# A fused sketch-attention and MLP kernel on one core: another token order, interleaved stages and other engines for the small steps

## The chip, the core and the metric

The kernel runs on one core of a Trainium2 chip. A core has a matrix engine (TensorE, in the profile PE for its matmuls and PEld for its weight loads), a vector engine (VectorE, DVE), an activation engine (ScalarE, ACT), GpSimd (POOL) and SyncE (SP), which here only issues transfers. Each engine works through its own list of instructions in order and waits at an instruction for semaphores. Matmuls write PSUM; DVE and ACT read it, POOL does not in this program. Transfers between HBM and the on-chip SBUF are issued from the queues of SP and ACT. The metric is the device time of one execution in microseconds (us).

## The reference, cut to what matters

Batch 4, heads H = 4, sequence 1088, head size D = 32, sketch size r = 8, model width 128 = H * D, hidden width 512. All data are float32 except S1, S2, w_ch1 and w_ch2, which are float64 and are rounded to float32 on the chip.

```python
def phi(x):
    a = np.einsum('rd,bhsd->bhsr', S1, x)
    b = np.einsum('rd,bhsd->bhsr', S2, x)
    return np.einsum('bhsi,bhsj->bhsij', a, b).reshape(*x.shape[:-1], r * r)
q_p, k_p = (phi(q), phi(k))
kv = np.einsum('bhsf,bhsd->bhfd', k_p, v)
z = np.sum(k_p, axis=2)
num = np.einsum('bhsf,bhfd->bhsd', q_p, kv)
den = np.einsum('bhsf,bhf->bhs', q_p, z)[..., None] + 1e-06
x = (num / den)                      # heads side by side: (batch, 1088, 128)
...
mu = np.mean(x, axis=-1, keepdims=True)
var = np.mean((x - mu) ** 2, axis=-1, keepdims=True)
xn = (x - mu) / np.sqrt(var + 1e-06) * g_ln
ch = np.maximum(xn @ w_ch1, 0.0) @ w_ch2
return (x + ch)
```

## The kernel before, in words

**Tiles.** A batch's 4 x 1088 rows of k or q are loaded as 128 partitions of 34 rows (`load_rows`, L99), v in six transfers a batch (`load_v`, L105). A chunk is 512 tokens of one batch, four tiles of 128; two chunks make 1024 tokens of a batch, and chunk 8 gathers the last 64 tokens of all four batches (two tiles). The order of instructions is written by hand (L547 to L625), and every engine follows it.

**Keys of a batch.** VectorE transposes 32x32 blocks of k into `kT` (`turn_k`, L250). TensorE multiplies by the sketches `sk` (L285, 36 matmul instructions for 9 tiles: each float32 matmul of the program is two instructions in the trace); ACT copies the features from PSUM tile `X` to `fs` (L290). The outer products `kp` (L294) run on GpSimd, those of the first four tiles of batch 0 on VectorE. `key_sums` (L301) forms z by 9 matmuls (L306), a mask (L312), a matmul (L318), and VectorE's copy into the query weights `skq` (L319). `key_values` (L324) contracts `kp` with v in 36 matmuls of 64 columns (L328); `key_spread` (L334) repeats the result over the partitions (ACT L336, PE L341) and VectorE copies it to `kvr` (L346).

**Queries of a chunk.** Transpose (`turn_q`, L262), features with z's denominators (`query_features`, L359, ACT copy L365), quotients on VectorE (L382 to L387), outer products `qp` on GpSimd (L391; chunk 0 on VectorE), a block transpose `qpT` on VectorE (L402), and `numerators` (L408): 32 matmuls of 32x32 weights and 128 columns (L425) into four banks of `X`, copied by ACT to `xT` (L434).

**MLP of a chunk.** `rows_of` (L439) transposes back to token rows `x`; `stats` and `roots` (L449, L460) take the variance on VectorE and 1/sqrt by an ACT square root and five small VectorE operations. `hidden` (L504) multiplies by `w1`, rounded, scaled by g and centred over its rows, in four parts through two PSUM tiles with ACT's ReLU into `hT`; `second` (L512) accumulates `hT` by `w2` into PSUM tile `PO`. `finish` (L521) scales each tile by 1/sqrt on ACT (L526), adds `x` on GpSimd (L529), and SP stores the chunk (L533); chunk 8 has four stores (L540). `weight1` and `weight2` (L477, L492) do the rounding, through `rounded` (L168).

**What sets the order around the change.** In the loop over chunks (L576) a chunk's four hidden matmuls, the numerators of the next chunk and its second matmuls follow one another, with query features two chunks ahead between the first and second hidden matmul; the key work of the next batch stands between chunks.

Of the kernel before, what the change touches and what calls it, by code (L numbers as in the profile page):

```python
# [25 lines left out]
def kernel(  # L26
# [27 lines left out]

    nc = tc.nc
# [24 lines left out]
    XP = ps.tile([P, 512], F32, name="XP")  # L80

# [5 lines left out]
    for i, src in enumerate((S1, S2)):  # L87
        nc.scalar.dma_start(
            out=s_raw[:, D * i : D * (i + 1)],
            in_=bass.AP(src.tensor, src.offset, [[0, P // R], [D, R], [1, D]]),  # L90
        )
# [40 lines left out]
    load_rows(kn, k, 1)  # L132
# [16 lines left out]
    head2 = const([P, H], I32, "head2")  # L149
    pool.iota(head2, [[2, H]], base=1, channel_multiplier=0)  # L150
# [11 lines left out]
    for t in kT:  # L162
        pool.memset(t[:, 8 * P + 64 :], 0.0)
    for t in vn:
        pool.memset(t[64:128, 8 * DM :], 0.0)


    def rounded(dst, raw, last, gain=None):  # L168

        n = raw.shape[-1]
        if raw.dtype == F32:
            last(raw, None)
            return
        words = raw.bitcast(U32)
        lo, hi = words[:, 0 : 2 * n : 2], words[:, 1 : 2 * n : 2]

        def temp(tag, dtype):
            return work.tile([P, n], dtype, tag=f"{tag}{n}", name=tag)  # L180
# [3 lines left out]
        dve.tensor_scalar(out=ex, in0=hi, scalar1=20, scalar2=0x7FF,
                          op0=ALU.logical_shift_right, op1=ALU.bitwise_and)
        dve.tensor_scalar(out=bits, in0=hi, scalar1=0xFFFFF, scalar2=None, op0=ALU.bitwise_and)

        act.activation(exf, ex, AF.Relu, bias=m896)
# [467 lines left out]
```

## Time and profile before

| | us |
|---|---|
| runs (three), median | 164.84 |
| lowest and highest run | 164.75, 166.06 |
| profiled execution, device time | 162.89 |
| its span, first to last instruction | 161.1 |
| PE busy in the span | 117.2 (73%) |
| DVE busy | 83.1 (52%) |
| ACT busy | 53.9 (33%) |
| POOL busy | 44.2 (27%) |
| mean granted TensorE clock | 0.922 |

A profile row names line, engine and operation, then out<-in, shapes and count; behind the bar stand the busy time, the mean ns of one, and the engine's idle time before it with what ended it. The times of engines overlap, so they don't add up to the span. The chain of waits is one path through all engines: it starts at the last instruction and goes back from each to what released it. A granted clock of 1.00 is full rate.

### The profile page before, as it was taken

What the parts mean: (1) busy time and instruction counts of PE and PEld (TensorE: products, weight loads), DVE (VectorE), ACT (ScalarE), POOL (GpSimd) and SP (SyncE); (2) the same over time, 40 slices, a digit from 0 to 9 for tenths busy, and PEclk for the clock granted to TensorE, in tenths of its full rate; (3) what the DMA queues carried; (4) which work ended last, traced back from release to release, by engine and by line L of the source; (5) the groups of instructions that cost most, each with busy time, mean ns of one, the idle gap of its engine ahead of it and who ended that gap; (6) DMA issues with size and microseconds to landing.
All of it is one profiled execution on the core that took longest, in us unless ns stands there. A gap on an engine that the chain in (4) does not pass through costs nothing.

```text
span 161.1 us, 3972 instructions
## 1 busy us (share of the span) xinstructions
PE 117.2 (73%) x1684; PEld 83.0 (52%) x1684; DVE 83.1 (52%) x243; ACT 53.9 (33%) x126; POOL 44.2 (27%) x45
## 2 busy tenths in 40 slices
PE   0047730483499773999999499999979999999700
PEld 0035630151439663549559354964954957669600
DVE  1173148439892638089396605766656666422210
ACT  0501013030615220262563224346245364552510
POOL 4035000004390340562340356333132232020300
PEclk9999999999569969699999857999999999999995
DMA  5998999300000020000020110001102002011020
GB/s 153 322 277 231 371 245 280 63 4 2 0 0 4 0 46 23 0 0 4 6 62 4 12 57 0 4 0 33 38 4 57 12 0 46 23 15 54 8 65 26
DMA packets 7049, 10.28 MB, mean 64 GB/s; under 512 B 2040, under 2 KB 4856, under 8 KB 7032
## 3 DMA queue, kind: packets, MB, share of 16 engines
q1 hardware_dynamic: 5928, 8.92, 20.2%
q10 hardware_dynamic: 1104, 1.11, 2.1%
q8 instruction: 13, 0.21, 0.6%
q14 instruction: 4, 0.03, 0.1%
HBM read 7.80 MB, written 2.23 MB: 62 GB/s over the span
## 4 chain that ended last, share of the span: by engine, by line
PE 60%; DVE 16%; ACT 10%; DMA 3%; issue 3%; POOL 1%; ACTq 1%; DVEq 0%; POOLq 0%
PE HP L509 20%; PE PO L514 14%; PE X L425 6%; PE X L359 5%; PE X L285 5%; DMA s_raw<-in_S_dram 3%; PE XP L443 2%; DVE st L454 2%; PE X L328 2%; ACT sc L526 2%; DVE kT L251 2%; ACT x L445 2%; DVE mv L455 2%; PE X L341 2%; PE PO L489 1%
## 5 line engine op out<-in xcount | busy, mean ns | idle before, releaser
L509 PE MATMUL HP<-xT,w 128*128 128x512 f32 (+1 forms) x72 | 38.1, 655 | 0.7 <-ACT hT L510 0.7
L514 PE MATMUL PO<-w,hT 128*128 128x128 f32 x272 | 34.0, 278 | 0.0
L514 PEld LDWEIGHTS PO<-w,hT 128*128 128x128 f32 x272 | 31.8, 192 | 1.5 <-issue 1.4
L510 ACT ACTIVATE hT<-HP 128x512 f32<-128x512 f32 (+1 forms) x36 | 20.4, 574 | 16.6 <-PE HP L509 16.6
L391 POOL TENSOR_TENSOR qp<-a,fq 128x1024 f32<-128x1024 f32 (+1 forms) x8 | 14.7, 1844 | 39.1 <-DVE a L387 25.1
L285 PE MATMUL X<-sk,kT 128*64 128x64 f32 x144 | 8.8, 296 | 19.2 <-DVE kT L251 14.7
L529 POOL TENSOR_TENSOR ob<-sc,x 128x512 f32<-128x512 f32 x8 | 10.1, 1266 | 44.7 <-issue 23.7
L509 PEld LDWEIGHTS HP<-xT,w 128*128 128x128 f32 x72 | 13.0, 209 | 13.4 <-ACT hT L510 7.0
L294 POOL TENSOR_TENSOR kp<-fs 128x2304 f32<-128x2304 f32 (+1 forms) x4 | 14.8, 3709 | 12.6 <-ACT fs L290 12.6
L285 PEld LDWEIGHTS X<-sk,kT 128*64 128x64 f32 x144 | 7.4, 199 | 21.1 <-DVE kT L251 13.4
L454 DVE BATCH_NORM_STATS2 st<-x 128x6 f32<-128x128 f32 x34 | 9.1, 268 | 14.3 <-ACT x L445 14.3
L382 DVE TENSOR_TENSOR ac<-fq 128x128 f32<-128x128 f32 (+1 forms) x9 | 4.7, 521 | 22.4 <-ACT fq L365 22.4
L526 ACT ACTIVATE sc<-PO,rstd 128x128 f32<-128x128 f32 x34 | 9.7, 367 | 11.2 <-DVE st L454 7.1
L402 DVE STREAM_TRANSPOSE qpT<-qp 128x1024 f32<-128x1024 f32 (+1 forms) x9 | 10.6, 1181 | 2.2 <-POOL qp L391 2.1
L425 PEld LDWEIGHTS X<-qpT,kvr 32*32 32x32 f32 x640 | 7.3, 106 | 8.3 <-issue 6.1
L359 PEld LDWEIGHTS X<-skq,qT 128*64 128x64 f32 x128 | 6.7, 160 | 7.8 <-DVE qT L265 3.8
L469 DVE TENSOR_TENSOR r<-r,r 128x4 f32<-128x4 f32 (+1 forms) x9 | 10.5, 1166 | 0.3
L425 PE MATMUL X<-qpT,kvr 32*32 32x128 f32 (+1 forms) x640 | 10.4, 275 | 0.0
L445 ACT COPY x<-XP 128x512 f32<-128x512 f32 (+1 forms) x9 | 5.1, 562 | 15.2 <-PE XP L443 15.2
L359 PE MATMUL X<-skq,qT 128*64 128x96 f32 x128 | 8.5, 284 | 1.8 <-DVE qT L265 1.2
L290 ACT COPY fs<-X 128x256 f32<-128x256 f32 (+1 forms) x8 | 3.2, 397 | 15.8 <-PE X L285 15.8
L489 PE MATMUL PO<-gw,ones 128*128 128x512 f32 x2 | 2.1, 1141 | 8.4 <-DVE gw L485 8.4
(76 smaller groups left out, 116.5 us busy)
## 6 DMA issues: line engine op xcount, KB each, us to landing
kn<-in_k_dram SPq DMA_DIRECT2D x4, 544.0 KB
qn<-in_q_dram SPq DMA_DIRECT2D x4, 544.0 KB
vn<-in_v_dram SPq DMA_DIRECT2D x16, 128.0 KB
out_dram<-ob SPq DMA_DIRECT2D x8, 256.0 KB
w_raw<-in_moe_w_ch_dram ACTq DMA_DIRECT2D x2, 512.0 KB
vn<-in_v_dram SPq DMA_DIRECT2D x8, 16.0 KB
out_dram<-ob SPq DMA_DIRECT2D x4, 32.0 KB
s_raw<-in_S_dram ACTq DMA_DIRECT2D x2, 32.0 KB
```

What stands on the lines that cost most here:

```text
L285: pe.matmul(X[64 * c : 64 * c + 64, base + W2R * t : base + W2R * (t + 1)], kT[b % 2][:, P * t + 64 * c : P * t + 64 * c + 64], sk, start= ...
L294: eng.tensor_tensor(out=_ap(o, 0, P, H * F * t0, [[F, (t1 - t0) * H], [R, R], [1, R]]), in0=_ap(f, 0, P, W2R * t0, [[2 * R, (t1 - t0) * H] ...
L359: pe.matmul(X[64 * i : 64 * i + 64, 1024 + WQ * t : 1024 + WQ * (t + 1)], src[:, P * t + 64 * i : P * t + 64 * i + 64], w, start=True, sto ...
L391: eng.tensor_tensor(out=_ap(p, 0, P, 0, [[F, m], [R, R], [1, R]]), in0=_ap(a2, 0, P, 0, [[R, m], [1, R], [0, R]]), in1=_ap(f, 0, P, R, [[R ...
L402: dve.transpose(_ap(t, 0, P, 0, [[32, n], [32 * n, 8], [1, 32]]), p[:, 0 : n * H * F])
L425: pe.matmul(X[D * h : D * h + D, o : o + 32 * m], kv[rows, DM * i + D * h : DM * i + D * h + D], t[rows, src : src + 32 * m], start=(i == ...
L454: dve.bn_stats(out=st[:, 6 * t : 6 * t + 6], in_=x[c][:, P * t : P * (t + 1)])
L469: dve.tensor_tensor(out=r1, in0=r1, in1=r0, op=ALU.mult)
L509: pe.matmul(hp[:, 0:n], w1[:, P * j : P * (j + 1)], xT[c][:, 0:n], start=True, stop=True)
L510: act.activation(hT[c][:, 512 * j : 512 * j + n], hp[:, 0:n], AF.Relu)
L514: pe.matmul(PO[:, DM * t : DM * (t + 1)], hT[c][:, 512 * j + P * t : 512 * j + P * (t + 1)], w2[:, DM * j : DM * (j + 1)], start=(j == 0), ...
L526: act.activation(sc[:, P * t : P * (t + 1)], PO[:, P * t : P * (t + 1)], AF.Copy, scale=rstd[c][:, t : t + 1])
```

## The change

**Token order.** A partition's 34 rows are now two runs of 17. A tile of 128 takes every run's t-th token, so kT, qT, v and the output use runs of 17: each 512-column transpose becomes two of 256 that write every second column, v comes in two transfers a batch, and the last tile is token 16 of each run.

**First chunk.** S1 and S2 are issued on two queues, w1 and w2 on SP behind batch 0. Three fill matmuls of zeros run at the start. Key products are all GpSimd's, in pieces; quotients of chunk 0 read PSUM; w1's low words go over ACT and GpSimd, and a matrix `center` (identity less 1/128) does the centring in one matmul.

**z on four tiles.** `key_sums` uses four column tiles of 32 instead of two of 64. **Numerators by batch.** From batch 1 on 32 matmuls serve both chunks, with 256 columns. **Powers on GpSimd.** 1/sqrt is an add and a power of -0.5. The quotient products go to GpSimd too; a ninth column of the sums holds 1e-6. **Residual on DVE.** Scale and add are one VectorE operation a tile, from PSUM. **New slots.** The order is written as two functions, `odd` and `even`, that put key and query work of the next batch between the MLP's matmuls.

```diff
-        for r in range(4):
-            nc.sync.dma_start(
-                out=_ap(vn[b], 32 * r, 32, 0, [[8 * D, H], [1, 8 * D]]),
...
+        for e in range(2):
+            n = (8 + e) * D
+            nc.sync.dma_start(
+                out=_ap(vn[b], 64 * e, 64, 0, [[NT * D, H], [1, n]]),
+                in_=bass.AP(v.tensor, base + 8 * e * D, [[U * D, 64], [S * D, H], [1, n]]),
...
+    load_s(nc.sync, 0, S1)
+    load_s(nc.scalar, 1, S2)
+    nc.scalar.dma_start(out=g_raw, in_=moe_g_ln.rearrange("(p o) -> p o", o=1))
     load_rows(kn, k, 0)
-    nc.scalar.dma_start(out=w1_raw, in_=moe_w_ch1)
     load_rows(qn, q, 0)
     load_v(0)
+    nc.sync.dma_start(out=w1_raw, in_=moe_w_ch1)
+    load_rows(kn, k, 1)
...
+    def turn(dst, off, src, t0, n):
+        for u in range(2):
+            dve.transpose(
+                _ap(dst, 0, P, off + u, [[64, 2], [P, n], [2, 32]]),
+                _ap(src, 0, P, U * D * u + D * t0, [[8 * D, 2], [D, n], [1, D]]),
+            )
...
         for t in range(NT):
-            c = t % 2
+            c = t % 4
             pe.matmul(
-                X[64 * c : 64 * c + 64, 1536:1568],
+                bank(bn, 32 * c, 32, 0, [[1, HR]]),
...
+        eng = pool if bn is None else dve
+        eng.tensor_tensor(
+            out=_ap(ac, 0, P, 0, [[9, m], [1, R]]), in0=_ap(f, 0, P, 0, groups),
...
+    def numerators(b, c0, c1):
+        src = qpT[b]
+        o, n = P * (c0 % 2), P * (c1 - c0)
...
+        pool.tensor_scalar(out=va[:, 0:n], in0=_ap(mv, 0, P, 1, [[2, n]]), scalar1=EPS,
+                           scalar2=None, op0=ALU.add)
+        pool.tensor_tensor(out=rs[:, 0:n], in0=va[:, 0:n], in1=half_power[:, 0:n], op=ALU.pow)
...
+        dve.scalar_tensor_tensor(
+            out=obs[c][:, P * t : P * (t + 1)],
+            in0=PO[:, P * t : P * (t + 1)] if src is None else src[:, 0:P],
+            scalar=rstd[c][:, t : t + 1], in1=x[c][:, P * t : P * (t + 1)],
+            op0=ALU.mult, op1=ALU.add,
+        )
...
+    fill(3, 512)
     turn_k(0, 0, 4)
+    key_features(0, 0, 4, 0)
...
+    def odd(b):
+        c, m = 2 * b + 1, b + 1
...
+        hidden(c, 0)
+        if m < B:
+            key_spread(m, 0)
+        hidden(c, 1)
+        hidden(c, 2)
+        hidden(c, 3)
+        if keys:
+            key_features(m + 1, 0, 4, 2)
+            key_features(m + 1, 4, NT, 3)
+            turn_q(2 * m + 2)
+            turn_q(2 * m + 3)
+        second(c, 0)
+        if keys:
+            key_sums(m + 1, 1)
...
+        second(c, 2)
+        last = 2 * m + (2 if m < B else 1)
+        numerators(m, 2 * m, last)
+        numerators_out(2 * m)
+        second(c, 3)
+        rows_of(2 * m)
...
+    def even(b):
+        c, m = 2 * b, b + 1
+        hidden(c, 0)
+        hidden(c, 1)
+        query_features(2 * m, 2)
...
+        hidden(c, 2)
+        hidden(c, 3)
+        if m < B:
+            query_features(2 * m + 1, 3)
...
+        rows_of(c + 1)
+        second(c, 0)
+        second(c, 1)
+        query_turn(2 * m)
+        stats(c + 1)
+        if m < B:
+            key_values(m, 1)
+            key_values_out(1)
+        second(c, 2)
+        second(c, 3)
```

How the instructions stand at three places. A row has the line, the operation, out<-in with the program's names (a number behind a name tells buffers apart), the size and a count.

TensorE from the first key values to the first hidden matmuls, before:

```order
L328 MATMUL X<-kp_190,vn_85 32x64 x36
L341 MATMUL X<-ident,kvT 128x128 x2
L359 MATMUL X<-skq_180,qT 64x96 x8
L489 MATMUL PO<-gw,ones 128x512
L425 MATMUL X<-qpT,kvr_194 32x128 x32
L443 MATMUL XP<-ident,xT 128x128 x4
L359 MATMUL X<-skq_180,qT 64x96 x8
L509 MATMUL HP_70<-xT,w_198 128x512
L285 MATMUL X<-sk,kT_149 64x64 x18
L509 MATMUL HP_71<-xT,w_198 128x512
```

The same stretch after:

```order
L410 MATMUL X<-skq,qT 64x32 x8
L410 MATMUL XP<-skq,qT 64x3x32 x8
L376 MATMUL X<-kp_176,vn_83 32x64 x36
L391 MATMUL X<-ident,kvT 128x128 x2
L628 MATMUL PO<-gw,center 128x512
L489 MATMUL X<-qpT,kvr_180 32x128 x32
L327 MATMUL PO<-sk,kT_133 64x2x32 x8
L547 MATMUL HP_70<-xT,w_184 128x512
L510 MATMUL XP<-ident,xT 128x128 x4
L547 MATMUL HP_71<-xT,w_184 128x512
```

The query features of chunks 0 and 1 now stand ahead of the key values, and the first eight key features of batch 1 ahead of the first hidden matmul.

VectorE in the first batch, from the key transposes on, before:

```order
L251 STREAM_TRANSPOSE kT_148<-kn_77 128x4x4x32 x2
L257 STREAM_TRANSPOSE kT_148<-kn_77 128x64
L236 TENSOR_TENSOR s2b<-s_f,m_140 128x128
L294 TENSOR_TENSOR kp_190<-fs_188 128x1024
L312 TENSOR_TENSOR zT<-X,m_140 128x32
L319 COPY skq_180<-X 128x4x8
L265 STREAM_TRANSPOSE qT<-qn_81 128x4x4x32
L346 COPY kvr_194<-X 128x256
```

And after:

```order
L287 STREAM_TRANSPOSE kT_132<-kn_75 128x2x4x32 x4
L293 STREAM_TRANSPOSE kT_132<-kn_75 128x2x32
L287 STREAM_TRANSPOSE qT<-qn_79 128x2x4x32 x4
L357 TENSOR_TENSOR zT<-X,m_124 128x32
L603 TENSOR_SCALAR g_187<-g_raw 128x1
L604 TENSOR_SCALAR g_188<-g_raw 128x1
L209 TENSOR_SCALAR ex<-w_raw 128x512
L368 COPY skq<-X 128x32
L217 TENSOR_SCALAR bits<-w_raw 128x512
L434 TENSOR_TENSOR ac_140<-fq,X 128x16x8
```

Key products and the copy of kvr have left VectorE, four half transposes of q came ahead of zT, and three steps of w1's rounding stand between zT and the copy of z's weights into skq.

TensorE in the steady stage, an odd chunk (chunk 1) with the keys of batch 2, before:

```order
L509 MATMUL HP_70<-xT,w_198 128x512
L359 MATMUL X<-skq_181,qT 64x96 x8
L509 MATMUL HP_71<-xT,w_198 128x512
L509 MATMUL HP_70<-xT,w_198 128x512
L509 MATMUL HP_71<-xT,w_198 128x512
L425 MATMUL X<-qpT,kvr_195 32x128 x32
L514 MATMUL PO<-w_199,hT 128x128 x8
L443 MATMUL XP<-ident,xT 128x128 x4
L514 MATMUL PO<-w_199,hT 128x128 x8
L306 MATMUL X<-fs_188 64x32 x9
L318 MATMUL X<-zT,s2b 128x32
```

And after:

```order
L547 MATMUL HP_70<-xT,w_184 128x512
L547 MATMUL HP_71<-xT,w_184 128x512
L327 MATMUL X<-sk,kT_132 64x2x32 x18
L552 MATMUL PO<-w_185,hT 128x128 x4
L352 MATMUL X<-fs_174 32x32 x9
L552 MATMUL PO<-w_185,hT 128x128 x4
L366 MATMUL X<-zT,s2b 128x32
L552 MATMUL PO<-w_185,hT 128x128 x4
L489 MATMUL X<-qpT,kvr_181 32x256 x32
L552 MATMUL PO<-w_185,hT 128x128 x4
L510 MATMUL XP<-ident,xT 128x128 x4
```

The key steps that stood between chunks now stand between the four parts of the second matmul, and the numerators have twice the columns and come once for two chunks.

More of the change, by code (lines that the diff above doesn't have):

```diff
@@ L203, with fill @@
     warm = const([P, 1], F32, "warm")
-    act.activation(warm, one, AF.Sqrt)
-    s_f = const([P, 2 * D], F32, "s_f")
-    def s_last(mant, scale):
-        if scale is None:
-            dve.tensor_copy(out=s_f, in_=mant)
-        else:
-            dve.tensor_tensor(out=s_f, in0=mant, in1=scale, op=ALU.mult)
-    rounded(s_f, s_raw, s_last)
+    act.activation(warm, one, AF.Relu)
+    def fill(n, cols):
+        for _ in range(n):
+            pe.matmul(PO[:, 0:cols], zeros[:, 0:P], zeros[:, 0:cols], start=True, stop=True)
@@ new lines, with round_s @@
+    s_f = const([P, 2 * D], F32, "s_f")
+    def round_s():
+        if s_raw.dtype == F32:
+            dve.tensor_copy(out=s_f, in_=s_raw)
+            return
+        r = Rounded(s_raw, "s")
+        r.exponent()
+        r.mantissa()
+        r.scale()
+        dve.scalar_tensor_tensor(out=r.mant, in0=r.lo, scalar=2.0**-52, in1=r.mant,
+                                 op0=ALU.mult, op1=ALU.add)
+        dve.tensor_tensor(out=s_f, in0=r.mant, in1=r.e3.bitcast(F32), op=ALU.mult)
+    round_s()
@@ new lines @@
+    query_features_out(1, XP_BANK)
+    query_quotients(0, 2)
+    query_products(0, 2, 4)
+    query_products(0, 0, 2, 2)
+    key_values_out(1)
+    key_spread(0, 0)
+    if weight1:
+        weight1.scale()
+        weight1.product(gw)
+    else:
+        dve.tensor_scalar(out=gw, in0=w1_raw, scalar1=g_raw, scalar2=None, op0=ALU.mult)
+    query_turn(0, 0, 2)
+    query_turn(0, 2, 4)
+    pe.matmul(PO, center, gw, start=True, stop=True)
+    numerators(0, 0, 1)
+    numerators_out(0)
+    act.copy(w1, PO)
@@ L569 @@
+    turn_k(1, 0, 4)
+    key_features(1, 0, 4, PO_BANK)
+    query_quotients(1)
+    query_products(1, 0, 4)
+    if weight2:
+        weight2.exponent()
+        weight2.mantissa()
+        weight2.low()
+        weight2.low_added()
+        weight2.scale()
+        weight2.product(w2)
+    else:
+        pool.tensor_copy(out=w2, in_=w2_raw)
     turn_k(1, 4, 4)
     turn_k_rest(1)
[L571 to L586 removed]
+    query_turn(1)
@@ L629 @@
+    odd(0)
+    for b in range(1, B):
+        even(b)
+        odd(b)
+    for j in range(JC):
+        hidden(8, j)
+    second(8, 0)
+    finish(8, 0)
+    second(8, 1, XP)
+    finish(8, 1, XP)
+    for b in range(B):
+        store_rest(b)
 _INS = ["q", "k", "v", "S1", "S2", "moe_g_ln", "moe_w_ch1", "moe_w_ch2"]
```

598 lines of the change are left out of this document (306 added, 292 removed).

## The prediction

> **What bounds the kernel now.** I read the granted clock and the engines' busy time by stage first, cut where the chain of waits changes its character: until chunk 0's transposed features are written, until chunk 1's first hidden matmul, until chunk 8's first hidden matmul, and the tail. A row has the stretch, its length, the busy time (and count) of TensorE's matmuls, its weight loads, VectorE, ACT and GpSimd, the granted clock, the DMA engines' share and GB/s.
>
> ```profile
> 0.00:34.44 34.44, 12.74 (x214) 9.27 (x214) 14.74 (x39) 5.64 (x11) 5.56 (x25) 1.00 0.80 227
> 34.44:65.48 31.04, 21.46 (x313) 15.83 (x313) 19.52 (x53) 8.76 (x20) 10.58 (x5) 0.81 0.04 10
> 65.48:148.22 82.74, 79.01 (x1135) 54.62 (x1135) 47.23 (x145) 36.33 (x84) 26.75 (x14) 0.95 0.08 21
> 148.22:161.10 12.88, 4.02 (x26) 3.27 (x24) 1.62 (x6) 3.17 (x11) 1.26 (x1) 0.82 0.12 31
> ```
>
> Stage three is TensorE's: 79.0 of 82.7 us. Stages one and two take 65.5 us and use TensorE for 34.2; no engine is full there, so a chain of latencies sets them. The chain of waits, in order of time (start, length, what), shows it, and gives the price of each step; of its 328 pieces, these:
>
> ```profile
> 0.74 0.63 ACTq L88
> 1.41 5.59 DMA s_raw<-in_S_dram
> 9.16 0.63 DVE kT L251
> 9.84 1.15 PE X L285 x16
> 11.43 1.39 PE X L285 x20
> 12.84 0.43 ACT fs L290
> 15.87 2.19 PE X L328 x72
> 19.83 0.43 DVE kvr L346
> 26.39 0.32 DVE ex L184
> 30.23 2.07 PE PO L489 x2
> 32.31 1.47 PE X L425 x63
> 33.80 0.59 ACT xT L434
> 40.31 0.72 ACT exf L188
> 43.77 4.46 PE HP L509 x6
> 54.42 0.42 PE X L318 x2
> 63.00 0.71 PE X L285 x16
> 79.62 2.87 PE HP L509 x6
> 82.49 1.00 PE X L425 x56
> 83.49 1.98 PE PO L514 x16
> 85.47 0.44 PE XP L443 x4
> 87.69 1.19 PE X L328 x72
> 89.39 0.72 PE X L341 x4
> 108.37 0.84 PE X L359 x16
> ...
> 143.01 1.39 PE X L425 x98
> ```
>
> Three things to see. S lands at 7.0 and nothing runs until then. From 20.3, where kvr ends, to 34.4 one thing follows another: query features, their quotients, then (26.4) the rounding of w1, then (30.2) the centring matmul, then numerators. And the first stage's matmuls run at about half rate although its clock reads 1.00: sixteen key-feature matmuls take 1.15 us at 9.84 and 0.71 at 63.00, 72 key-value matmuls 2.19 against 1.19, and six hidden ones 4.46 at 43.77 against 2.87 at 79.62.
>
> **Start of the change: S to key values.** Both halves of S are issued on ACT's queue, beside kn on SP's. The change puts one on each, ahead of kn. An undisturbed small transfer is bounded by SyncE's wait for the last stores:
>
> ```profile
> SPq L651 <- DMA out_dram<-ob: 3.6, 2, 3.0
> ```
>
> So S lands between 7.0 (no gain) and 0.74 + 0.63 issue + 3.0 = 4.4; I take 4.4, since nothing of size is ahead of it. The rounding to sk keeps its 2.1 us (7.0 to 9.16): 6.5. The transposes become halves with every second column written; no row shows that form. These do bound it:
>
> ```profile
> L265 DVE STREAM_TRANSPOSE qT<-qn 128x512 f32<-128x512 f32 x8 | 5.5, 694 | 0.0
> L271 DVE STREAM_TRANSPOSE qTr<-qn 128x64 f32<-128x64 f32 x4 | 0.8, 202 | 0.0
> L391 POOL TENSOR_TENSOR qp<-a,fq 128x1024 f32<-128x1024 f32 x7 | 13.7, 1954 | 37.9 <-DVE a L387 25.1 <-DVE r L467 12.8
> L391 DVE TENSOR_TENSOR qp<-a,fq 128x1024 f32<-128x1024 f32 x1 | 1.2, 1224 | 0.0
> L391 POOL TENSOR_TENSOR qp<-a,fq 128x512 f32<-128x512 f32 x1 | 1.1, 1067 | 1.2 <-DVE r L467 1.2
> ```
>
> A line through 202 ns at 64 and 694 at 512 gives 0.41 us for 256; the ends are 0.35 (half the long one) and 0.69 (stride costs a factor two). Taken 0.41: 0.8 for the first pair, 7.3. The three fill matmuls are six instructions of 1.04 (30.23: 2.07 for two) from about 1.2, so TensorE is free at 7.4, just in time; their worth is that the key matmuls run at the warm rows. Then 0.71 and the copy (8.5), twenty more at 0.89 and the copy (9.9), the first query features beside it, 18 sums at the key features' warm rate (0.8; four column tiles taken as no gain, the ends are 0.2, all four at once, and 1.3, the cold rate of 9.84) to 10.8, zT 0.2, the 0.42 of z's weights: 11.4. Then VectorE must copy z's weights, behind w1's first rounding steps. Here the change adds a risk. All four key products go to GpSimd: three of 1.07 and one of some 1.5 (line through the two GpSimd rows), 8.5 to 13.2, where VectorE took the first 1024 columns (1.2) beside GpSimd with the rest. And the timeline shows what a running GpSimd instruction does to VectorE:
>
> ```profile
> 44.32 4.15 POOL L294 TENSOR_TENSOR kp<-fs 128x2304 f32<-128x2304 f32 x1
> 45.73 2.77 DVE L457 TENSOR_SCALAR va<-mv 128x4 f32<-128x4 f32 x1
> 54.04 0.17 DVE L457 TENSOR_SCALAR va<-mv 128x4 f32<-128x4 f32 x1
> ```
>
> The same small operation takes 0.17 alone and 2.77, until GpSimd ends, beside it. So w1's first steps, 0.6 alone by what w1's exponent takes at 26.39, cost up to 2.4 (until the last key product); taken 1.2: 12.6. They also need w1, which moves to SyncE's queue behind kn, qn and v of batch 0: 2.2 MB at stage one's 227 GB/s land it at 10.5, a microsecond ahead; kn and v come well before their use. Query features (1.1), key values 1.19, copy 0.4, spread 0.72, copy 0.4: kvr at 16.4 (was 20.3).
>
> GPSIMD Engine Reference (the Trainium skill, Key points and Engine selection) says that GpSimd shares its SBUF interfaces with VectorE, in contention when a VectorE instruction uses two ports or two SBUF inputs, and that elementwise work is about twice as fast on VectorE. It speaks against these moves. The rows agree on the blocking; for the speed they show 1954 against 1224 ns, and by the page's factor of two on 1224 the four pieces would end at 14.1 instead of 13.2, some 0.4 into the key values, an estimate that would make the sum 133.4.
>
> **First chunk to its features.** Quotients and half the products of chunk 0 now read PSUM beside the key values. w1: exponent, mantissa and low part on ACT (0.7 each from 12.4: 14.5), then GpSimd's sum (1.3), half of chunk 0's products (1.07), VectorE's two scale steps squeezed between (0.7), the product 1.3: 18.8. Centring 1.1 to 2.1, numerators 1.1 to 1.5, copy 0.59: 22 to 23; I take 23.5 with something for a cold clock (was 34.4; ends 20 and 28).
>
> **Chunk 0 to chunk 1.** Before, chunk 0's later hidden matmuls waited until 43.8 behind batch 1's keys, whose transposes stood late on VectorE and whose copies stood behind w2's rounding on ACT; after that statistics, z, query features, products and spread of batch 1 followed one another until 65.5. Now TensorE's work in this stretch is: w1 copy 0.6, key features 1.6, hidden 3.8, rows 0.9, sums 0.8, z 0.4, numerators 1.1, second 4.0, query features 1.7, key values 1.2: 16.1. I add 1.6 for a cold clock (4.46 less 2.87) and 1.8 because w2's three ACT passes stand ahead of the first ReLU: 19.5. Chunk 1 starts at 43.0 instead of 65.5.
>
> **The steady stage.** From 79.0 busy: a mean clock of 0.95 is 8 us at half rate, 4.1 lost if TensorE was busy in all of it; less 2.8, since in part it waited. Numerators for 256 columns once a batch instead of 128 twice, 64 instructions either way. The wide form has no row: it costs 1.0 if the rate of instructions limits it, 2.0 if the columns do. The 128 narrow ones of chunk 8, 32 columns each, speak for the first: 1.39 at 143.01 for 98 of them, 14 ns apart, against 1.00 for 56, 18 apart, at four times the columns. Taken 1.07: less 2.9 in three batches (0 to 3.0). Query features of chunk 3 leave (-0.8), keys of batch 2 and a spread come in (+1.6, +0.7): 74.8. What stands between is hidden work: scaling (34 ACTIVATEs) and the residual (eight GpSimd adds) become 34 VectorE operations of 128 elements (0.2 to 0.7, the rows of 64 and 512; some 0.3), which take 10 us of VectorE's 35 idle ones, and lengthen the wait for the PSUM bank by no more than the four scalings did; roots leave ACT and VectorE for two GpSimd instructions a chunk; the quotient products go to GpSimd, some 0.4 each by its line. Two new waits per batch (keys' second half behind the first copy, rows behind the numerators' copy): 0.5 each, 2 in all: 77.
>
> GpSimd's power of 128x4 has no row: the nearest is VectorE's 0.17 for 128x4, the far end GpSimd's 1.95 us for a whole query product. Its result is due some 8 us later, so either costs nothing.
>
> **Tail.** The last four stores are issued from 154.18 on; the span ends at 161.1.
>
> ```profile
> L526 ACT ACTIVATE sc<-PO,rstd 128x128 f32<-128x128 f32 x34 | 9.7, 367 | 11.2 <-DVE st L454 7.1 <-PE PO L514 4.1
> 154.18 2.22 SPq L540 DMA_DIRECT2D out_dram<-ob  x4
> ```
>
> Four stores go out one after the other; now two on each of two queues: -1.1. The last ReLUs no longer stand behind four scalings of 0.37 on ACT, which overlap a little (-1.1), and two scalings and an add become one short operation (-0.7): 10.
>
> **Sum.** 23.5 + 19.5 + 77 + 10 = 130.0 against 161.1. The profiled execution took 162.89, 1.8 more than its span: 131.8. The median of the runs, 164.84, is 1.2% above the profiled one: 133.
>
> **The rivals.** (1) The start stays long: GpSimd's run of products holds w1's and w2's rounding on VectorE, and the clock falls back. For it: the 2.77 row, and clock 0.81 in stage two. Each of the four stretches of VectorE rounding waits up to 2.4 (+6), and 16 us of TensorE work at half rate adds up to 5 more than I put in; against: most of it overlaps. With two thirds of it: 140. TensorE: Matmul & The Clock Gate (the Trainium skill, Part 1) has the clock fall to half after an idle window of about 3.4 us and return after a busy one; by that rule, a fill that ends at 7.4 would not outlast the wait for w1. No run here shows the fill; the half-rate rows agree. (2) The steady stage is not TensorE's: the interleaved slots wait for ACT and GpSimd, as the 31 us of stage two did. At 2.5 us a batch and 1 us a chunk: +12, 144. Against it: ACT and GpSimd are under half busy there. (3) Everything overlaps, the clock stays up: 19 for stage one, 17 for two, 75, 9: 123. (4) Not faster: the strided half transposes. Ten stand ahead of the first key values and features, eight a batch later, and no row has their form. Each extra us of one costs 9 or so at the start. In the steady stage VectorE is busy 47 of 83 us, 14 of a batch's 24. At about 2.2 us apiece (1.8 more than taken) the start loses 16, and a batch gains 14 on VectorE, 4 more than there is room for, 13 in three: the 30 saved are gone, 163. Below that the kernel is faster. Against it: this is five times the line through the rows.
>
> **How the numbers follow.** My forecast (128 to 138) 0.55; rival (1) 0.20; (2) 0.11; (3) 0.08; (4) 0.06. The range 126 to 143 leaves out (4), half of (3) and the worse half of (2). All but (4) lie far below 163, so faster by over 1%, about what a measurement of this kernel can tell, 0.93; within 1% 0.02; slower 0.05.
>
> **What would show it.** S landing near 4; the first key features at 0.7 for sixteen; chunk 0's features copied near 23 and chunk 1's first hidden near 43; 32x256 numerators at 1.1 us for 64; a TensorE row of nines from 43 to the end; a DVE transpose of 128x256 near 0.41. A transpose over 1 us, VectorE rounding rows over 1 us, or hidden matmuls of chunk 0 at the rate of 43.77 would show me wrong.

## The result and the profile after

The changed kernel takes 138.06 us (median of four runs, 136.94 to 138.93) where the kernel before took 164.8 beside it: a ratio of 0.840, 95% interval 0.830 to 0.850. The profiled execution took 136.94, with a span of 135.2, 1.7 around it. The ratios leave out executions that were disturbed (two of s_one_queue's four, its profiled one among them, of which only the first 10 us are read, two of residual_on_act's, and three of the kernel before beside the last four kernels); the medians do not.

First the granted clock and busy time by stage of the changed kernel, cut at the prediction's four places (columns as there: stretch, length, TensorE's matmuls, its weight loads, VectorE, ACT, GpSimd, clock, DMA share, GB/s).

```profile
0.00:26.52 26.52, 16.64 (x252) 9.69 (x252) 13.87 (x45) 7.08 (x15) 14.38 (x30) 0.83 0.93 272
26.52:43.85 17.33, 16.51 (x273) 12.06 (x273) 7.64 (x28) 8.07 (x15) 9.47 (x9) 0.87 0.17 37
43.85:124.66 80.81, 75.08 (x973) 54.10 (x968) 34.28 (x124) 29.14 (x56) 34.68 (x39) 0.96 0.08 25
124.66:135.20 10.54, 3.85 (x24) 3.08 (x23) 2.44 (x10) 1.89 (x5) 0.95 (x2) 0.92 0.16 39
```

Against before the stages lose 7.9, 13.7, 1.9 and 2.3 us: the gain is made ahead of chunk 1's first hidden matmul. Against the forecast of 23.5, 19.5, 77 and 10 they are off by +3.0, -2.2, +3.8 and +0.5. The longer of the two misses can be seen in the page's picture of the span in 40 slices (tenths of TensorE's busy time, and of its granted clock):

```profile
PE   5963924699999923899999989999999999999900
PEclk9999595559999996589999999999999999999997
```

The 15th and 16th slice (47 to 54 us) hold a 2 and a 3 in the middle of the nines, and the clock reads 6, 5 and 8 from the 16th to the 18th. The chain of waits names what ended late there (start, length, what):

```profile
42.42 0.23 POOL va L524
...
42.73 1.02 POOL rstd L526
43.75 0.44 POOL ac L434
...
45.36 1.95 POOL qp L456
47.31 0.42 POOL ac L434
...
48.91 1.96 POOL qp L456
...
50.90 1.25 DVE qpT L469
52.14 0.66 DVE kT L287 x2
...
52.85 1.15 PE X L327 x16
...
55.78 2.01 PE PO L552 x8
```

Chunk 1's hidden matmuls are done at 48.1 and TensorE wants batch 2's key features next. Their rows (kn, long landed) are to be transposed by VectorE, where that stands behind the transposes of chunk 2's and chunk 3's products; and those wait for two rounds of quotients and products, one after the other on GpSimd, behind chunk 1's power. TensorE is idle for 4.75 us, and what follows runs at half rate (called cold here, and full rate warm): 1.15 us for sixteen key features (0.69 elsewhere), 2.01 for eight second-layer matmuls (1.09 at 61.94). From 63.47 on, the chain is TensorE's almost alone.

The timeline of the start shows the other miss (start, length, engine, line, what; in brackets the idle time before it and what ended it):

```profile
11.99 1.20 DVE L209 TENSOR_SCALAR ex<-w_raw 128x512 uint32<-128x512 uint32 x1 [0.35 <-DMA w_raw<-in_moe_w_ch_dram]
...
17.46 0.29 DVE L434 TENSOR_TENSOR ac<-fq,X 128x128 f32<-128x128 f32 x1 [3.84 <-PE X L376]
...
19.51 0.37 ACT L383 COPY kvT<-X 128x256 f32<-128x256 f32 x1 [3.74 <-DVE qp L456]
...
22.36 2.08 PE L628 MATMUL PO<-gw,center 128*128 128x512 f32 x2 [1.71 <-POOL gw L239]
```

The quotients of chunk 0, whose features were there at 14.0, start when the last key-value matmul (L376) ends; the key values' copy, whose matmuls ended at 17.4, starts when VectorE's product ends; and the weights gw, whose scale steps stand behind those quotients, end at 22.3.

### The profile page after: what moved, and what is told of

Read it like the earlier page. It is cut to its first block, busy times and chain, and to the rows that moved or that the text cites. A ratio compares the mean times of both kernels' runs of the same rounds, so it can differ in the third digit from the quotient of the medians.

```text
span 135.2 us, 3549 instructions
## 1 busy us (share of the span) xinstructions
PE 112.1 (83%) x1514; PEld 78.9 (58%) x1514; DVE 58.2 (43%) x206; ACT 46.2 (34%) x90; POOL 59.5 (44%) x79
## 4 chain that ended last, share of the span: by engine, by line
PE 70%; DVE 7%; POOL 6%; DMA 6%; ACT 2%; SPq 2%; issue 1%; ACTq 0%; DVEq 0%; POOLq 0%
PE PO L552 23%; PE HP L547 21%; PE X L489 6%; DMA w_raw<-in_moe_w_ch_dram 6%; PE X L410 4%; PE X L376 3%; PE XP L510 3%; PE X L327 3%; POOL qp L456 3%; PE PO L628 2%; POOL gw L239 1%; SPq L119 1%; DVE qpT L469 1%; PE XP L410 1%; SPq L110 1%
## 5 line engine op out<-in xcount | busy, mean ns | idle before, releaser
L547 PE MATMUL HP<-xT,w 128*128 128x512 f32 (+1 forms) x72 | 34.7, 602 | 0.1
L340 POOL TENSOR_TENSOR kp<-fs 128x768 f32<-128x768 f32 (+3 forms) x12 | 17.9, 1512 | 9.6 <-ACT fs L332 9.6
L564 DVE SCALAR_TENSOR_TENSOR ob<-PO,rstd,x 128x128 f32<-128x128 f32 x33 | 9.2, 338 | 22.7 <-issue 14.7
L501 ACT COPY xT<-X 128x512 f32<-128x512 f32 (+1 forms) x9 | 5.1, 564 | 23.6 <-PE X L489 23.6
L327 PE MATMUL X<-sk,kT 128*64 128x64 f32 x108 | 5.4, 259 | 6.4 <-DVE kT L287 5.0
L526 POOL TENSOR_TENSOR rstd<-va,half_power 128x4 f32<-128x4 f32 (+1 forms) x9 | 8.9, 994 | 0.7
L489 PE MATMUL X<-qpT,kvr 32*32 32x256 f32 (+2 forms) x448 | 8.5, 320 | 0.3 <-DVE skq L368 0.3
L410 PEld LDWEIGHTS X<-skq,qT 128*64 128x64 f32 x128 | 5.3, 137 | 5.4 <-ACT hT L548 3.0
L410 PE MATMUL X<-skq,qT 128*64 128x96 f32 (+2 forms) x128 | 6.6, 246 | 1.9 <-DVE skq L368 1.3
L521 DVE BATCH_NORM_AGGREGATE mv<-st 128x2 f32<-128x6 f32 x34 | 6.2, 182 | 1.2
L191 PE MATMUL PO<-zeros 128*128 128x512 f32 x6 | 5.5, 1088 | 1.4 <-DVE bit L164 1.4
```

What stands on the lines that cost most here:

```text
L327: pe.matmul(bank(bn, 64 * c, 64, HR * (t - t0), [[HR * n, 2], [1, HR]]), kT[b % 2][:, P * t + 64 * c : P * t + 64 * c + 64], sk, start=Tru ...
L340: pool.tensor_tensor(out=_ap(o, 0, P, H * F * t0, [[F, n], [R, R], [1, R]]), in0=_ap(f, 0, P, HR * t0, [[R, n], [1, R], [0, R]]), in1=_ap( ...
L410: pe.matmul(bank(bn, 64 * i, 64, P * s0 + HR * t, [[P, s1 - s0], [1, HR]]), src[:, P * t + 64 * i : P * t + 64 * i + 64], skq[:, w + HR * ...
L489: pe.matmul(bank(r, D * h, D, o + o2, [[1, m]]), kv[rows, DM * i + D * h : DM * i + D * h + D], src[rows, 256 * (2 * h + i) + o + o2 : 256 ...
L526: pool.tensor_tensor(out=rs[:, 0:n], in0=va[:, 0:n], in1=half_power[:, 0:n], op=ALU.pow)
L547: pe.matmul(hp[:, 0:n], w1[:, P * j : P * (j + 1)], xT[c][:, 0:n], start=True, stop=True)
```

## The experiments

Twelve kernels. The first three are edits of the changed kernel, three_orders is all three together, and the other eight are edits of three_orders. They ran in three groups, the first on one chip and the other two on another (medians of before: 164.73, 163.75, 163.29), so the ratio to before is the better comparison between groups; a difference of 0.01 in it (1.6 us) is the least that stands out.

| kernel | median us | ratio to before (95%) |
|---|---|---|
| changed kernel | 138.06 | 0.840 (0.830 to 0.850) |
| keys2_ahead | 131.39 | 0.801 (0.793 to 0.809) |
| w1_ahead | 133.15 | 0.811 (0.803 to 0.820) |
| kv_own_bank | 133.48 | 0.813 (0.806 to 0.821) |
| three_orders | 126.47 | 0.771 (0.764 to 0.778) |
| no_fill | 126.69 | 0.775 (0.769 to 0.781) |
| narrow_numerators | 127.82 | 0.782 (0.776 to 0.788) |
| residual_on_act | 132.39 | 0.803 (0.795 to 0.812) |
| further_orders | 126.05 | 0.771 (0.764 to 0.777) |
| s_one_queue | 130.60 | 0.795 (0.787 to 0.804) |
| twice_turned | 132.59 | 0.815 (0.809 to 0.821) |
| further_orders2 | 125.35 | 0.771 (0.766 to 0.777) |
| powers_on_act | 141.29 | 0.868 (0.862 to 0.874) |

### keys2_ahead: the hole is VectorE's order

```diff
     stats(1)
+    turn_k(2, 0, 4)
+    turn_k(2, 4, 4)
+    turn_k_rest(2)
+    turn_q_rest(0)
+    turn_q_rest(1)
     query_quotients(2)
...
     query_turn(3)
-    turn_k(2, 0, 4)
-    turn_k(2, 4, 4)
-    turn_k_rest(2)
-    turn_q_rest(0)
-    turn_q_rest(1)
```

> The transposes of batch 2's key rows stand on DVE ahead of chunk 2's quotients and no longer behind chunks 2 and 3's product transposes. Theory A (DVE's order makes TensorE's hole of 4.75 us at 48.1 to 52.9, since those transposes stand behind two serial chains of quotients and products on GpSimd): key features of batch 2 start within 0.5 us of chunk 1's last hidden matmul, the hole, its 0.5 us after the first copy and the half-rate work behind it (about 2 us) go, and the time is 130 to 133. Rival B (GpSimd's chain is late for everything): the hole moves to batch 1's numerators, which need chunk 3's products transposed at 52.1, or to the key sums, and the time is 135 to 138.

Theory A held: 131.39. TensorE's timeline, from chunk 1's last hidden matmul on:

```profile
47.66 0.69 PE L327 MATMUL X<-sk,kT 128*64 128x64 f32 x16
48.82 0.80 PE L327 MATMUL X<-sk,kT 128*64 128x64 f32 x20 [0.47 <-ACT fs L332]
...
53.23 0.41 PE L366 MATMUL X<-zT,s2b 128*128 128x32 f32 x2 [1.13 <-DVE zT L357]
...
54.54 1.50 PE L489 MATMUL X<-qpT,kvr 32*32 32x256 f32 x64
```

The key features follow without a wait and at the full rate. The 0.47 behind the first copy, which theory A had going, stays, and a smaller wait of 1.13 for z comes up; the numerators, which rival B saw waiting for chunk 3's products, don't wait. GpSimd's chain was late only for what had been queued behind it.

### w1_ahead and kv_own_bank: the two waits of the start

w1_ahead moves the scale and product of w1's rounding ahead of chunk 0's quotients, and the centring matmul ahead of the spread:

```diff
         weight1.low_added()
+        weight1.scale()
+        weight1.product(gw)
     query_features_out(1, XP_BANK)
     query_quotients(0, 2)
     query_products(0, 2, 4)
     query_products(0, 0, 2, 2)
+    pe.matmul(PO, center, gw, start=True, stop=True)
     key_values_out(1)
     key_spread(0, 0)
-    if weight1:
-        weight1.scale()
-        weight1.product(gw)
...
-    pe.matmul(PO, center, gw, start=True, stop=True)
```

> The scale and the last product of w1's rounding stand ahead of chunk 0's quotients and products on DVE and GpSimd, and the centring matmul ahead of the spread key values on TensorE. Theory A (w1's rounding, behind the quotients, ends the wait before the first numerators): weights gw end near 18 in place of 22.3, the centring runs in TensorE's idle stretch, the numerators start near 21.3, xT(0) is written near 23.3 in place of 26.5, and the time falls by 2.5 to 3.5 to about 135. Rival B (the quotients, which wait for the key values, end it by themselves): xT(0) not before 25 and the time falls by less than 1.5. Rival C (chunk 0's early gain is lost at the hole before batch 2's key features, because that hole is timed by the statistics of chunk 1 and GpSimd): xT(0) moves but the time by under 1.

kv_own_bank leaves the order and gives batch 0's key values and their spread other PSUM tiles:

```diff
-    BANKS = [(X, 0), (X, 512), (X, 1024), (X, 1536), (PO, 0), (XP, 0)]
+    BANKS = [(X, 0), (X, 512), (X, 1024), (X, 1536), (PO, 0), (XP, 0), (HP[0], 0), (HP[1], 0)]
...
-    key_values(0, 1, 0, 4)
-    key_values(0, 1, 4, NT)
+    key_values(0, 6, 0, 4)
+    key_values(0, 6, 4, NT)
...
-    key_values_out(1)
-    key_spread(0, 0)
+    key_values_out(6)
+    key_spread(0, 7)
```

> Batch 0's key values and their spread go into the two hidden banks, idle until chunk 0's hidden matmuls, in place of the four-bank tile that the quotients read. Theory A (chunk 0's quotients wait for the key values' last matmul, 3.84 us, and the key values' copy for the DVE products, 3.74 us, only because all sit in one PSUM tile): the first quotient starts at 14 to 15.5 in place of 17.46, the copy of the key values at 17.5 in place of 19.51, the numerators 1.5 to 3 earlier, the time 135 to 136.5. Rival B (the quotient waits for the matmuls in any case, by TensorE's order): it still starts after 17.3 and the time stays within 0.7 of the changed kernel.

Both theories held, and both gains, 4.9 and 4.6 us between the medians, came out larger than expected; between the profiled spans they are 3.9 and 3.0. The timelines, first of w1_ahead, then of kv_own_bank:

```profile
18.19 1.13 PE L623 MATMUL PO<-gw,center 128*128 128x512 f32 x2 [1.06 <-POOL gw L239]
...
20.92 1.07 PE L489 MATMUL X<-qpT,kvr 32*32 32x128 f32 x64 [0.46 <-ACT kvr L395]
...
48.37 1.01 PE L327 MATMUL X<-sk,kT 128*64 128x64 f32 x16 [4.77 <-DVE kT L287]
```

```profile
14.58 0.29 DVE L434 TENSOR_TENSOR ac<-fq,X 128x128 f32<-128x128 f32 x1 [0.50 <-PE X L410]
...
17.94 0.37 ACT L383 COPY kvT<-HP 128x256 f32<-128x256 f32 x1 [1.62 <-PE HP L376]
```

In w1_ahead xT(0) is written at 22.6 in place of 26.5. 1.4 us of the excess are TensorE's rate: the centring takes 1.13 instead of 2.08 and the numerators 1.07 instead of 1.47, with shorter waits ahead of them. The hole keeps its length (4.77) and shifts by the whole 4.5 us, so rival C, that it would swallow the gain, falls. In kv_own_bank the quotient waits for its own matmuls (L410) and the copy for the key values: the waits were for the tile X, not for data. Both edits cut the same stretch, so their gains should not add, and they don't: the next version gains 11.6, as much as keys2_ahead and w1_ahead together.

### three_orders

> All three of the edits before. If the start is bound by the two waits and the middle by DVE's order, as the theories say: xT(0) written at 21 to 23.5, no hole above 1 us after chunk 1's hidden matmuls, time 126 to 130. If the start's gain is lost in a later wait (rival): no better than the transposes alone, within 1 us of it.

126.47, inside the first theory's band; one wait above 1 us is left after chunk 1's hidden matmuls, the 1.13 for z. The stages, cut at the same places as above:

```profile
0.00:22.31 22.31, 15.49 (x252) 10.12 (x252) 13.61 (x45) 7.06 (x15) 13.18 (x30) 0.85 0.92 272
22.31:39.05 16.74, 14.97 (x272) 10.77 (x272) 9.15 (x35) 7.88 (x15) 10.63 (x10) 1.00 0.42 107
39.05:114.15 75.10, 72.98 (x973) 52.08 (x967) 32.53 (x118) 29.16 (x56) 34.64 (x39) 1.00 0.08 27
114.15:124.80 10.65, 4.02 (x26) 3.25 (x24) 2.56 (x10) 1.90 (x5) 0.95 (x2) 0.85 0.15 38
```

From chunk 1 on TensorE is busy for 73.0 of 75.1 us at clock 1.00: the forecast's steady stage (74.8 and two more) is what this order gives, and the changed kernel's 80.8 was that and the hole.

### s_one_queue: the split of S, by itself

```diff
-    load_s(nc.sync, 0, S1)
+    load_s(nc.scalar, 0, S1)
```

> The version with the three orders, with both halves of S issued on ACT's queue again. Theory A (the split onto two queues is what brings S from 7.0 to 3.2, and the first key transposes stand behind S's rounding on VectorE): the rounding starts at 6 to 7, the first key features at 9 to 10 in place of 7.04, and 2 to 2.8 us reach the end, 128.5 to 129.3. Rival B (w1's landing at 11.9 and GpSimd's key products cover most of it): the key features move as much but the time by under 1. Rival C (the place ahead of kn, not the second queue, brings S early): S lands before 4.5 and nothing moves.

The two runs behind the ratio took 129.11 and 129.47, 2.8 above three_orders, by the ratio 0.024 (3.9 us). The timeline, to set beside 3.20 and 7.04 in three_orders:

```profile
7.08 0.20 DVE L209 TENSOR_SCALAR ex<-s_raw 128x64 uint32<-128x64 uint32 x1 [5.11 <-DMA s_raw<-in_S_dram]
...
9.82 1.11 PE L327 MATMUL X<-sk,kT 128*64 128x64 f32 x16 [2.54 <-DVE kT L287]
```

Theory A held. The split brings S 3.9 us earlier; 2.8 of it reach the key features, since kn's transposes then wait for kn (6.2) and not for S, and as much reaches the end.

### twice_turned: the fourth rival's price

```diff
-        for u in range(2):
+        for u in (0, 1, 0, 1):
```

> The version with the three orders, with every half transpose of key and query rows done twice (0.41 us more for each of 34 pairs' halves). Theory A (the prediction's rule for the fourth rival: each microsecond more of one half transpose costs about nine at the start, nothing in the steady stage): 0.4 times 9, some 3.5 us at the start, 129 to 131. Rival B (w1's landing covers the first query transposes, and only the first key pair and the place behind chunk 3's products are on the path): 0.8 at the start and up to 1.6 before batch 2's z, 127.3 to 129. Rival C (VectorE becomes the bound in the steady stage): over 131.

132.59, 0.044 in the ratio: the size of rival C, but none of the three places. First its hidden matmuls of chunk 0 and 1, batch 2's z and chunk 2's hidden; then the same hidden matmuls in three_orders:

```profile
23.57 1.13 PE L547 MATMUL HP<-xT,w 128*128 128x512 f32 x2
...
40.47 1.13 PE L547 MATMUL HP<-xT,w 128*128 128x512 f32 x2
...
52.50 0.64 PE L366 MATMUL X<-zT,s2b 128*128 128x32 f32 x2 [3.42 <-DVE zT L357]
...
54.93 2.38 PE L489 MATMUL X<-qpT,kvr 32*32 32x256 f32 x64
...
59.21 1.88 PE L547 MATMUL HP<-xT,w 128*128 128x512 f32 x4
```

```profile
23.46 1.12 PE L547 MATMUL HP<-xT,w 128*128 128x512 f32 x2
...
39.05 1.12 PE L547 MATMUL HP<-xT,w 128*128 128x512 f32 x2
...
52.97 1.88 PE L547 MATMUL HP<-xT,w 128*128 128x512 f32 x4
```

The doubled transposes cost 0.1 us at the start (w1's landing at 11.9 covers them), 1.3 in chunk 0's stage, 4.8 in chunk 1's, where batch 2's z waits for VectorE and TensorE then falls to half rate, and 0.2 in all that is left. So the prediction's rule for its fourth rival (nine times the excess, at the start) is wrong in its place; VectorE's tight stretch is the one between 24 and 53 us, where chunks 0 and 1 also have the keys of batches 1 and 2.

### residual_on_act and powers_on_act: the moves that the prediction priced low

residual_on_act puts the scaling back on ACT and the addition on GpSimd:

```diff
-        dve.scalar_tensor_tensor(
-            out=obs[c][:, P * t : P * (t + 1)],
...
+        act.activation(
+            obs[c][:, P * t : P * (t + 1)],
...
+            scale=rstd[c][:, t : t + 1],
+        )
+        if t == n - 1:
+            (pool if c < 8 else dve).tensor_tensor(
```

> The version with the three orders, with scaling by ACT (one ACTIVATE for 128 elements, 34 of them) and the addition by GpSimd (VectorE for chunk 8), as before the change, in place of 34 VectorE operations. Theory A (the steady stage is TensorE's and ACT has room; only the tail pays): no new wait over 0.3 us a chunk on TensorE, +0.5 to +2 in all. Rival B (the scalings stand ahead of the next chunk's ReLUs on ACT, so each third hidden matmul waits for its bank): 0.5 or more of new wait per chunk, +4 or more, 130.5 to 135.

The ratio rises by 0.032 (5 us; 4.1 between the profiled spans). The size is rival B's, the place is only partly so. Three rows of its timeline:

```profile
42.25 1.27 POOL L571 TENSOR_TENSOR ob<-ob,x 128x512 f32<-128x512 f32 x1
...
49.79 0.41 PE L366 MATMUL X<-zT,s2b 128*128 128x32 f32 x2 [2.36 <-DVE zT L357]
...
118.37 1.13 PE L547 MATMUL HP<-xT,w 128*128 128x256 f32 x4 [0.92 <-ACT hT L548]
```

The addition (1.27) stands on GpSimd between chunk 2's product and chunk 3's quotient, so the chain of the hole is longer by 1.2 and batch 2's z is that much later. In the steady batches TensorE waits for ReLUs three times, 0.8 together; another 0.9 is in the tail, where the last ReLUs stand behind four scalings. By stage the profiled execution loses 1.2 us in chunk 1, 1.3 from chunk 2 to chunk 7 and 1.8 in the tail, and gains 0.2 at the start.

powers_on_act puts the square root on ACT and the rest on VectorE, but leaves the addition of epsilon (va) on GpSimd, which before the change was VectorE's; so it is the old operations in the new places, not the old code. It also warms ACT up with the square root instead of ReLU; both traces have one table load of ACT (1.28 us), at the start:

```diff
-        pool.tensor_tensor(out=rs[:, 0:n], in0=va[:, 0:n], in1=half_power[:, 0:n], op=ALU.pow)
+        act.activation(r1, va[:, 0:n], AF.Sqrt)
+        dve.reciprocal(r0, r1)
+        dve.tensor_tensor(out=r1, in0=va[:, 0:n], in1=r0, op=ALU.mult)
...
```

> The version with the three orders, with the inverse roots as before the change: ACT's square root, then five small VectorE operations, in place of one GpSimd power of 1.03 us. Theory A (the result is due late, so neither form is on the path, as the prediction says): within 0.7 of 126.5. Rival B (ACT's root waits for the statistics and stands ahead of the next chunk's ReLUs, so hidden matmuls wait for their bank): 0.4 or more of new wait a chunk on TensorE, 130 or more. Rival C (the power of 1.03 is itself on GpSimd's chain before chunks 2 and 3's products): faster by 0.5 to 1.1.

141.29, 15 us more: rival B, and more than it foresaw. Chunk 0's statistics end at 29.3; then:

```profile
28.44 4.32 POOL L340 TENSOR_TENSOR kp<-fs 128x1024 f32<-128x1024 f32 x2
...
32.84 0.23 POOL L524 TENSOR_SCALAR va<-mv 128x4 f32<-128x4 f32 x1
...
33.10 0.21 ACT L527 ACTIVATE r<-va 128x4 f32<-128x4 f32 x1 [5.04 <-POOL va L524]
...
33.34 0.18 DVE L528 RECIPROCAL r<-r 128x4 f32<-128x4 f32 x1 [4.08 <-ACT r L527]
...
35.19 0.64 PE L366 MATMUL X<-zT,s2b 128*128 128x32 f32 x2 [5.21 <-DVE zT L357]
```

va is queued behind the key products; the root holds ACT, and with it the ReLUs, for 5.04 us; the reciprocal holds VectorE for 4.08; z comes late and TensorE waits 5.21. Up to chunk 1's first hidden matmul this costs 6.8 us. Chunk 1 loses 4.2: the roots stand on VectorE ahead of the transposes of batch 2's keys and of chunk 2's quotients, GpSimd waits 3.04 for those, and TensorE 2.46 for batch 2's z, with half rate behind it. The rest loses 3.9; there TensorE waits four times for ReLUs, 4.8 together. The power takes 1.03 on GpSimd, as long as the root and the five operations together (0.21 and 0.83), yet behind it only GpSimd waits. How much the old operations would cost with va on VectorE was not tried.

### narrow_numerators and no_fill: two small parts

```diff
-        numerators(m, 2 * m, last)
+        for c1 in range(2 * m, last):
+            numerators(m, c1, c1 + 1)
```

> The version with the three orders, with the numerators of batches 1 to 3 formed per chunk again (64 matmuls of 128 columns, twice) in place of 64 of 256 columns. The wide form took 1.42 to 1.50 and the narrow warm one 1.07. Theory A (the steady stage is TensorE's, so TensorE's work is the price): +0.65 a batch, +1.9 in three, 128 to 129. Rival B (the prediction's 2.9 for three batches): 129 to 130. Rival C (other waits hide it): within 0.7 of 126.5.

127.82; the ratio is 0.011 up, 1.4 to 1.8 us. That is near theory A (1.9) and below the prediction's 2.9; rival C can't be excluded by the intervals. The traces speak for theory A's mechanism at a lower price: the 128 narrow matmuls of a batch take 1.90 us where the 64 wide ones took 1.49, so 1.2 in three batches, and the profiled spans differ by 1.2.

```diff
-    fill(3, 512)
```

> The version with the three orders, without the three fill matmuls at the start. Theory A (the fill lifts TensorE's rate for the first key features, and these are on the chain): the first sixteen key features take about 1.15 us in place of 0.69 and the twenty 1.4 in place of 0.80, the eighteen sums 0.6 in place of 0.38, and the time rises by 0.8 to 1.5 from 126.5. Rival B (w1's landing at 11.9 sets the start in any case): the matmuls slow down alike but the time rises by less than 0.5.

126.69, no difference that can be told: rival B. TensorE's timeline without the fill:

```profile
7.06 1.12 PE L327 MATMUL X<-sk,kT 128*64 128x64 f32 x16 [7.06 <-DVE kT L287]
8.65 1.33 PE L327 MATMUL X<-sk,kT 128*64 128x64 f32 x20 [0.47 <-ACT fs L332]
```

These are slower, as expected (0.69 and 0.80 with it), but the key values, 2.15 with the fill, take 1.83 without: with it TensorE is at half rate again by then. w1's landing covers the difference.

### further_orders and further_orders2

The first loads w1 ahead of v of batch 0, takes w1's exponent ahead of z, puts chunk 0's products into one VectorE operation, and moves the second half of the key features behind a second-layer tile, sums, z and query transposes later.

```diff
+    nc.sync.dma_start(out=w1_raw, in_=moe_w_ch1)
     load_v(0)
-    nc.sync.dma_start(out=w1_raw, in_=moe_w_ch1)
...
-    query_products(0, 2, 4)
-    query_products(0, 0, 2, 2)
+    query_products(0, 0, 4, 2)
...
             key_features(m + 1, 0, 4, 2)
+        second(c, 0)
+        if keys:
             key_features(m + 1, 4, NT, 3)
```

> The version with the three orders and five more: w1 loaded ahead of v of batch 0; w1's exponent ahead of z on VectorE; both halves of chunk 0's products in one VectorE operation; the second half of the key features behind the first second-layer tile and the sums and z a tile later; the query transposes behind the sums. If the remaining waits (w1's landing at 11.9, 1.30 for z's copy, 1.13 for z in batch 2, 0.47 for each key copy) are on the path: gw at 16 to 17, numerators at 19 to 19.8 in place of 20.6, no z wait in batch 2, time 122 to 125. If they were hidden (rival): 126 to 127. If v now lands too late for the key values (rival): these start after 16 and the time is over 126.5.

126.05, within the rival's band, but not all of it was hidden: batch 2's z no longer waits, and chunk 2's first hidden matmul comes at 51.79 instead of 52.97, of which the profiled span keeps 0.9, too little for the runs to tell. At the start nothing moved: w1 lands two microseconds sooner, but its mantissa bits then run on VectorE beside a key product on GpSimd (1.19 instead of 0.41), and gw ends at 17.6 where it ended at 18.0.

The second adds:

```diff
-    key_products(0, 6, NT)
...
     turn_q(1)
+    key_products(0, 6, NT, dve)
...
-    pe.matmul(PO, center, gw, start=True, stop=True)
     key_values_out(6)
     key_spread(0, 7)
+    pe.matmul(PO, center, gw, start=True, stop=True)
```

> The further orders with two edits: the last piece of batch 0's key products on VectorE in place of GpSimd, and the centring matmul behind the spread key values again. In the run before these, the mantissa bits of w1 took 1.19 beside a running key product on GpSimd and gw ended at 17.6, with TensorE waiting 1.74 for it and the key values' spread queued behind. If that is the path: bits in 0.41, gw at 16.5 to 17, numerators at 18.1 to 18.8 in place of 19.7 to 20.7, time 124 to 125.3. Rival (the numerators then wait for the products' transposes or a later wait takes it): 125.5 to 126.5.

125.35; the ratio is three_orders' (0.771). The bits took 0.42, but VectorE's key product took 1.60 beside GpSimd's and moved z 1.3 us later, and the numerators, begun at 19.3, ended at 21.4 against 21.7. Inconclusive between the two; the start has more than one chain of this length. All three versions, three_orders with three edits the simplest, beat both the kernel before and the changed one.

## Why the prediction was right, and where it was not

The time lies in the range, 5 us above the value and just past the band of 128 to 138 that had the largest chance. The mechanism held in the main: start shortened, chunk 1 brought forward by 21.6 us (65.48 to 43.85, said 43.0), then TensorE's stage. Two of the signs named as showing it wrong came all the same: a VectorE rounding row over 1 us (w1's exponent, 1.20), and chunk 0's first hidden matmuls at half rate (2.08 us for two, 1.12 in three_orders). They cost microseconds, not the mechanism, and part of the closeness is luck, since errors cancel in the second and third stage. The step that failed most is one that I took as free.

- **S at 4.4.** It landed at 3.2, but kn, landing at 6.2, became the limit; that the key features began at 7.1 (said 7.4) is luck. The split alone is worth 2.8 us, where I had 0 to 2.6.
- **Half transposes at 0.41.** They took 0.41 (four in 1.43, overlapping). Rival 4 needed 2.2.
- **The start at 23.5, with kvr at 16.4 and gw at 18.8.** It was 26.5, 21.0 and 22.3. "Quotients and half the products of chunk 0 now read PSUM beside the key values" is the sentence that failed: they did not run beside them but after them, since both use the tile X (kv_own_bank). Of the 4.6 us by which kvr was late, this wait is 2.1; query features and key values at half rate (1.9 and 2.12 us, said 1.1 and 1.19) are 1.7, and the rest is w1, which landed at 12.0 instead of 10.5. The margins for GpSimd holding VectorE (1.2) were right: w1's exponent took 1.20 beside the key products.
- **The second stage at 19.5.** It took 17.3. The addition for a cold clock (1.6) was needed: the three groups from 27.05 took 1.13, 2.08 and 1.06, in three_orders 0.69, 1.12 and 0.60, so 1.9 more. The 1.8 for w2's ACT passes was not, and TensorE's own work, 14.7 without the half rate, was less than the 16.1 counted.
- **The steady stage at 77.** Two new waits a batch of 0.5 were counted, but not the order on VectorE in chunk 1: 4.75 us of hole and 1.9 of half rate (0.46, 0.54 and 0.92 for three groups behind it). Taking it away gave 6.7 us. The stage is only 3.8 over the forecast because the rest of the sum was too long: without the hole it takes 75.1 (three_orders). In that same chain stands the power, of which I said "due some 8 us later, so either costs nothing": its 1.02 us (42.73) lie ahead of chunk 2's quotients.
- **The 2.9 us of the wide numerators.** The wide form took 1.42 where I took 1.07; the three batches were worth 1.2 (traces) to 1.8 (ratio).
- **The residual, hidden in the steady stage and 1.8 in the tail.** The operations took 0.338 (said 0.3). In the orders of three_orders the whole move is worth 4 to 5 us: the tail's 1.8 came as said, but the steady stage gains too, 1.2 of it because a GpSimd addition leaves the chain before batch 2's z.
- **The fill.** I gave it the warm rate of the matmuls up to the key values; it came for the key features and sums but not for the key values, and was worth nothing (no_fill).
- **Tail at 10**: 10.5. **From the profiled run to the median**, 1.2%: 0.8%.

Rival 1 was partly real: the rate did fall back at the start, and GpSimd held w1's exponent for some 0.8 us, but the longest wait came by the tile X. Rival 2, a steady stage in which slots wait for other engines, happened once, in chunk 1. TensorE: Matmul & The Clock Gate (the Trainium skill, Part 1) has the rate fall after an idle window of about 3.4 us. These traces agree only in part. Waits of 3.42, 4.75 and 5.21 us are followed by half rate, and those of 1.13 and 2.36 (residual_on_act) are not; but so is one of 2.46 (powers_on_act: 2.38 for the wide numerators, 1.49 in three_orders). And at the start of three_orders the rate falls at 13.2 behind waits of at most 1.30, where TensorE had been busy for 1.5 of 4.3 us (granted clock 0.50 from there to 17.4); so the fill did not last to the key values.

## What to carry to other kernels

On an engine that serves its queue in order, place work whose data has long landed ahead of the instruction that waits for another engine: seven short transposes, moved up, were worth 6.7 us on an engine that is 43% busy. Look at which PSUM tile two steps share before counting them as parallel: steps in separate banks of one tile waited for each other here. A small operation is priced by the queue that stands behind it, not by its duration: a power of 1.03 us on GpSimd beat a root and five operations of the same sum, whose waits stood ahead of ReLUs and transposes.

## What the runs showed of the hardware

A half transpose that writes every second column costs no more than the line through the plain ones (0.41 us for 128x256). GpSimd's elementwise power of 128x4 took 1.03 us, where its addition of the same size took 0.22. Numerators in 32x32 tiles: 64 matmuls with 256 columns took 1.49 us where 128 with 128 columns took 1.90 (three_orders and narrow_numerators, the same place). Some VectorE operations are held by a running GpSimd product: w1's exponent began at 11.57 to 13.04 in the changed kernel, keys2_ahead, w1_ahead, kv_own_bank, three_orders and no_fill, and each time it ended 0.28 or 0.29 us after GpSimd's last key product (0.52 to 1.36 us long, where w2's, begun while GpSimd was idle, took 0.36); the mantissa bits of further_orders ended 0.29 after (1.19 instead of 0.41). Others were not: in three_orders the reciprocal (0.25) and the product that reads PSUM (0.69) kept their times beside GpSimd's sum for w1 (15.3 to 16.6).
